# Three banks of one PSUM tile against three tiles of one bank each

## The chip, the cores and the metric

The kernel runs on one core of one Trainium2 chip. The metric is the device time in microseconds (us) of one execution; lower is better. The engines are TensorE (PE in the profile, with its weight loads apart as PEld), VectorE (DVE), ScalarE (ACT), GpSimd (POOL) and SyncE (SP, which issues the DMAs).

## What is computed

A chunked linear scan over 4 batches, 8 heads and 768 positions gives a matrix x of 3072 rows and 256 columns. Behind it stands a gated feed-forward block:

```python
y[:, :, sl] = y_intra + y_inter                   # scan, chunk by chunk
state = decay_full * state + np.sum(Bx, axis=2)
...
x = attn_out.transpose(0, 2, 1, 3).reshape(B * S, H * D)     # 3072 x 256
gate = 1.0 / (1.0 + np.exp(-(x @ w_gate)))        # w_gate, w_val: 256 x 1536
val = x @ w_val
return gate * val @ w_out                         # w_out: 1536 x 256
```

## The kernel before

Positions are taken in six chunks of 128 per batch. The scan of a chunk makes the chunk's columns of x, and the feed-forward block of an earlier chunk runs on TensorE meanwhile. Every fp32 product is made of three matmuls on operands that are split into a high and a low part (high by high, high by low, low by high).

The last two chunks are joined and are taken last. Their two feed-forward inputs are one block matrix of 2 x 2 blocks, and each product with a weight tile is made by a scheme of seven products instead of eight, on sums and differences of blocks (`joined_tasks`, L1456). There are twelve groups, `group(i)`, i from 0 to 11: the even ones multiply by w_gate, the odd ones by w_val. A group has seven products n of three matmuls of 128 x 512 each, all on L1362, in the order 1, 7, 2, 6, 4, 5, 3 (the last group: 1, 7, 6, 2, 5, 3, 4). Their moving operand tells them apart in the trace: products 1 and 2 are `gv<-x,w`, product 4 is `gv<-xt,w`, products 5, 6 and 7 are `gv<-xt,s`, product 3 is `gv<-xb,s`.

The products of a group go to three banks of PSUM, a, d and b. Products 1, 6, 5 and 3 are accumulated in a, products 7 and 4 in d, product 2 goes to b. Odd groups have a and b exchanged (`bank_of`, L1340), so that product 1 of a group goes to the bank that the group before leaves free. A group's results are read out by `corner(i, n)`:

- L1395, ACT: a copy out of the bank into a tile c, behind product 1 (corner 11), product 7 (corner 22) and product 6 (corner 21). The bank goes on being accumulated behind it.
- L1397, DVE: another bank is added to that copy, behind product 2 (b, corner 11), product 4 (d, corner 21) and product 5 (a, corner 22).
- L1400, ACT: the sigmoid of an even group's corner, in place. L1384, ACT: that of corner 12, straight out of the bank, behind product 3. L1388, DVE: corner 12 of an odd group, out of the bank times the sigmoid.
- L1404, DVE: an odd group's corner times the sigmoid.

`h_parts` splits each product of gate and value into two parts for the second matrix product (L1414, a cast on ACT or DVE; L1416, a subtraction on POOL or DVE), and `out_of` multiplies them by w_out (L1438, `acc<-w,h`, six matmuls of 256 columns a step, eight steps per two groups). `s_block(i)` makes the sums of weight blocks for group i: L1319 (`ww`, on POOL or DVE), L1326 (four of `sw`, DVE), L1329 (ACT), L1331 (POOL or DVE).

The order of the instructions on every engine is written out by hand in a list, `ORDER`, of entries such as `pe.group7` or `act.corner7_11`. Between engines, semaphores are placed by the framework, from the tiles that the instructions read and write: an instruction waits for those ahead of it in the program's order that touch the same tile. The three banks are slices of one tile of four banks, `gv`, which the pool `ps_cb` gives (L1358); that pool held the scan's tile of four banks before. So accesses to different banks of `gv` by different engines are kept in the program's order as well.

Of the kernel before, what the change touches and what calls it, by code (L numbers as in the profile page):

```python
# [8 lines left out]
F32 = mybir.dt.float32  # L9
# [5 lines left out]
PSUM = bass.MemoryType.PSUM  # L15
# [183 lines left out]
def tile_ssd_then_gated_ffn(  # L199
# [16 lines left out]
    P = 128  # L216
# [22 lines left out]
    dr = ctx.enter_context(tc.tile_pool(name="dr", bufs=1, space=DRAM))  # L239
    ps_mm = ctx.enter_context(tc.tile_pool(name="ps_mm", bufs=3, space=PSUM))  # L240
    ps_y = ctx.enter_context(tc.tile_pool(name="ps_y", bufs=1, space=PSUM))
    ps_cb = ctx.enter_context(tc.tile_pool(name="ps_cb", bufs=1, space=PSUM))


    ctx.enter_context(tc.manual_schedule(engines=None))
# [10 lines left out]
    for i in range(WARM):  # L256
        n = 4 if i < WARM - 1 else 3
# [59 lines left out]
    def step(eng, cost, needs=(), makes=(), port=False, **buffers):  # L317

        return eng, cost, needs, makes, port, buffers
# [928 lines left out]
    x7, s7, hj, bank, temps = {}, {}, {}, {}, {}  # L1248

    def x_part(name, part):  # L1250

        if name in ("b11", "b21"):
            if ("x5", part) not in x7:
                x7["x5", part] = wk.tile([P, NK, 512], F32R, tag=("xh", "xl")[part], name=f"x5{part}")
            return x7["x5", part][:, int(name == "b21")]
        if name not in x7:
            pool, tag = {"b22": (hp, "r0"), "t1": (wk, "xh"), "t2": (wk, "xl"), "t3": (wk, "bct"), "t4": (wk, "bct")}[name]
            x7[name] = pool.tile([P, 2, 512], F32R, tag=tag, name=f"x{name}")
        return x7[name][:, part]
# [73 lines left out]
    def standing(i, n):  # L1333

        if n in (1, 2, 4):
            k, f = {1: (0, 0), 2: (1, 0), 4: (1, 1)}[n]
            return [wgv[i][:, part, k, f * P : (f + 1) * P] for part in range(2)]
        return [s_part(i, part)[:, {5: 0, 6: 1, 7: 2, 3: 3}[n]] for part in range(2)]

    def bank_of(i, n):  # L1340

        return bank["gv"][:, "adb".index(n) if i % 2 == 0 or n == "d" else "bda".index(n)]

    def group(i):

        last = i - 1
        free = lambda k: [(k, last)] if i else []
        for n in (1, 7, 6, 2, 5, 3, 4) if i == NF - 1 else (1, 7, 2, 6, 4, 5, 3):
            needs = [("x7", MOVING[n], late) for late in range(2)] + ([("s7", i)] if n in (3, 5, 6, 7) else [])
            needs += {  # L1350
                1: free("b"), 7: free("d"), 2: free("a"), 6: [("s1", i)], 4: [("p7", i)], 5: [("u2", i)], 3: [("u4", i)]
            }[n]
            if i == 0:
                needs += [("sum", 2 * T1 + 1), ("pfirst", 2 * T1 + 1)]
            made = [("p", n, i)] + ([("done", i // 2)] if n == (4 if i == NF - 1 else 3) and i % 2 else [])
            yield step("pe", 3 * 0.227, needs, made, port=12)
            if "gv" not in bank:
                bank["gv"] = ps_cb.tile([P, 4, 512], F32, tag="pcb", name="gv")  # L1358
            out = bank_of(i, {1: "a", 6: "a", 5: "a", 3: "a", 7: "d", 4: "d", 2: "b"}[n])
            (wh, wl), (xh, xl) = standing(i, n), [x_part(MOVING[n], part) for part in range(2)]  # L1360
            for m, (one, two) in enumerate(((wh, xh), (wh, xl), (wl, xh))):
                nc.tensor.matmul(out, one, two, start=m == 0 and n in (1, 7, 2), stop=m == 2, skip_group_check=True)  # L1362
# [12 lines left out]
    def corner(i, n):  # L1375

        gate = i % 2 == 0
        free = [("free", nth(i, n) - 8)] if nth(i, n) > 7 else [("h", T2 - 1, f) for f in range(NF - 3, NF)]
        if (i, n) in ((0, "12"), (1, "11")):
            free += [("x7", k, late) for k in ("b22", "t1", "t2", "t3") for late in range(2)]  # L1380
        if n == "12":
            if gate:
                yield step("act", ACT_MM, [("p", 3, i)] + free, [("a", i), ("sig", i, n)])
                nc.scalar.activation(temp(i, n), bank_of(i, "a"), AF.Sigmoid)  # L1384
                return
            yield step("dve", DVE_MM, [("p", 3, i), ("sig", i - 1, n)], [("a", i), ("hf", i // 2, n)])
            g = temps[i - 1, n]
            nc.vector.tensor_tensor(out=g, in0=bank_of(i, "a"), in1=g, op=ALU.mult)  # L1388
            return
        product, of, copied, last, also, freed = {  # L1390
            "11": (1, "a", "s1", 2, "b", "b"), "22": (7, "d", "p7", 5, "a", "u4"), "21": (6, "a", "u2", 4, "d", "d"),
        }[n]
        yield step("act", ACT_MM, [("p", product, i)] + free, [(copied, i)])
        t = temp(i, n)
        nc.scalar.copy(t, bank_of(i, of))  # L1395
        yield step("dve", DVE_MM, [("p", last, i)], [(freed, i)])
        nc.vector.tensor_tensor(out=t, in0=bank_of(i, also), in1=t, op=ALU.add)  # L1397
        if gate:
            yield step("act", ACT_SB, [], [("sig", i, n)])
            nc.scalar.activation(t, t, AF.Sigmoid)  # L1400
            return
        eng = yield step(("dve", "pool"), (DVE_MM, 1.29), [("sig", i - 1, n)], [("hf", i // 2, n), ("free", nth(i, n))], port=True)
        g = temps[i - 1, n]
        engines[eng].tensor_tensor(out=g, in0=t, in1=g, op=ALU.mult)  # L1404
# [51 lines left out]
    def joined_tasks(t):  # L1456

        for late in range(2):
            for n in MOVING.values():
                task(t - 20.0 + 3 * late, f"x{n}_{late}", x_block(n, late))  # L1460
        for i in range(NF):
            at = t + 7.5 * i
            task(at - 12.0, f"s{i}", s_block(i))
            task(at, f"group{i}", group(i))
            for n, d in (("11", 0.9), ("22", 1.7), ("21", 3.0), ("12", 7.5)):
                task(at + d, f"corner{i}_{n}", corner(i, n))
        for j in range(NF // 2):
            for m, n in enumerate(PLACES):
                task(t + 15.0 * j + (11.0, 14.0, 16.0, 17.0)[m], f"part{j}_{n}", h_parts(j, n))
                task(t + 15.0 * j + (15.0, 18.0, 21.0, 24.0)[m], f"out{j}_{n}", out_of(j, n))  # L1470
        for k in (T2, T1):
            for at in range(2):
                task(t + 110.0 + (k == T1), f"rows{k}_{at}", stored_rows(k, at))
# [371 lines left out]
```

## Time and profile before

| | us |
|---|---|
| median of 3 runs (lowest to highest) | 407.23 (403.02 to 408.65) |
| the profiled execution, its own time | 404.01 |
| span of the profiled execution | 402.2 |
| TensorE busy | 361.2 (90%) |
| VectorE busy | 242.4 (60%) |
| ScalarE busy | 167.0 (42%) |
| GpSimd busy | 174.9 (43%) |

The span is the time from the first to the last instruction. Busy shares are means over stages of different kinds. Matmuls are pipelined, and the ends of a matmul are modelled: in rows of several, the distance of the starts tells the pace. The last stage runs from the first `gv` matmul at 251.87 us to the end of TensorE's work at 396.64 us.

### The profile page before, as it was taken

How to read it: one execution, taken by the hardware profiler on the slowest of the kernel's cores; microseconds unless marked ns; L12 is line 12 of the kernel's file. 1: busy time of each engine (PE TensorE's matmuls, PEld its weight loads, DVE VectorE, ACT ScalarE, POOL GpSimd, SP SyncE). 2: the span in 40 equal slices, each digit the busy share in tenths (PEclk: the TensorE clock that was granted, in tenths of full speed). 3: DMA queues.
4: the chain of work that ended last, by engine and by line, in shares of the span. 5: the costliest groups of instructions: out<-in, count | busy, mean ns of one | idle time of the engine just before them, and what ended most of it. 6: DMA issues, size and time to landing. Idle time of an engine off the chain costs nothing.

```text
span 402.2 us, 8260 instructions
## 1 busy us (share of the span) xinstructions
PE 361.2 (90%) x3328; PEld 279.9 (70%) x3328; DVE 242.4 (60%) x425; ACT 167.0 (42%) x315; POOL 174.9 (43%) x174
## 2 busy tenths in 40 slices
PE   8999999999999999999999997877778777787884
PEld 4676677878888888888888876546566655565674
DVE  7786878774467566552224589837495483818264
ACT  2577754368743135541044432432523333232321
POOL 5364776468975415662055464131362250302011
PEclk9999999999999999999999998999996999999999
DMA  8989844364624434420011000002000000000003
GB/s 169 266 201 256 292 137 117 76 100 117 132 75 95 93 73 80 113 55 13 18 38 29 15 2 2 0 1 45 9 0 0 0 2 0 0 2 0 0 2 104
DMA packets 87467, 27.43 MB, mean 68 GB/s; under 512 B 75718, under 2 KB 80262, under 8 KB 87430
## 3 DMA queue, kind: packets, MB, share of 16 engines
q1 hardware_dynamic: 82982, 26.26, 27.2%
q10 hardware_dynamic: 4448, 0.66, 1.0%
q8 instruction: 26, 0.43, 0.4%
q14 instruction: 11, 0.09, 0.1%
HBM read 23.46 MB, written 3.44 MB: 67 GB/s over the span
## 4 chain that ended last, share of the span: by engine, by line
PE 72%; DVE 14%; ACT 5%; issue 2%; POOL 1%; DMA 0%; DVEq 0%; ACTq 0%; POOLq 0%
PE gv L1362 15%; PE pg L1243 14%; PE pv L1243 14%; PE po L1497 9%; PE po L1535 6%; PE acc L1438 5%; ACT c L1395 4%; DVE c L1397 3%; DVE c L1404 2%; PE pv L1139 1%; PE banks L783 1%; PE banks L767 1%; PE pg L1139 1%; DVE h L1414 1%; DVE xt L1291 1%
## 5 line engine op out<-in xcount | busy, mean ns | idle before, releaser
L1210 POOL TENSOR_TENSOR h<-g,h 128x512 fp32r<-128x512 f32 x36 | 50.0, 1390 | 56.4 <-ACT h L1208 54.4
L1243 PE MATMUL pg<-xh,w 128*128 128x512 f32 x168 | 59.6, 395 | 0.0
L1243 PE MATMUL pv<-xh,w 128*128 128x512 f32 x168 | 58.9, 391 | 0.1
L1397 DVE TENSOR_TENSOR c<-gv,c 128x512 f32<-128x512 f32 x36 | 24.3, 688 | 55.7 <-PE gv L1362 42.6
L1497 PE MATMUL po<-h,w 128*128 128x512 f32 x216 | 52.1, 398 | 0.0
L1204 DVE TENSOR_TENSOR g<-pv,g 128x512 f32<-128x512 f32 x36 | 24.9, 691 | 41.9 <-PE pv L1243 40.9
L1497 PEld LDWEIGHTS po<-h,w 128*128 128x128 f32 x216 | 41.2, 192 | 9.0
L1416 POOL TENSOR_TENSOR h<-c,h 128x512 fp32r<-128x512 f32 x11 | 16.4, 1489 | 71.0 <-ACT h L1414 52.8
L1438 PEld LDWEIGHTS acc<-w,h 128*128 128x128 f32 x288 | 40.1, 195 | 3.6 <-DVE h L1416 0.4
L1362 PE MATMUL gv<-xt,s 128*128 128x512 f32 x108 | 33.7, 421 | 8.9 <-ACT c L1384 4.2
L1395 ACT COPY c<-gv 128x512 f32<-128x512 f32 x36 | 20.4, 587 | 51.0 <-PE gv L1362 46.3
L1438 PE MATMUL acc<-w,h 128*128 128x256 f32 x288 | 40.9, 287 | 0.2 <-DVE h L1416 0.2
L1183 ACT ACTIVATE g<-pg 128x512 f32<-128x512 f32 x44 | 26.3, 598 | 29.7 <-PE pg L1243 29.3
L1208 ACT CAST h<-g 128x512 fp32r<-128x512 f32 x35 | 21.7, 620 | 38.4 <-DVE g L1204 38.4
L1243 PEld LDWEIGHTS pg<-xh,w 128*128 128x128 f32 x168 | 31.5, 188 | 7.9 <-DVE h L1200 0.7
L1243 PEld LDWEIGHTS pv<-xh,w 128*128 128x128 f32 x168 | 31.5, 188 | 7.2 <-POOL w L495 0.5
L1243 PE MATMUL pg<-xl,w 128*128 128x512 f32 x84 | 32.7, 390 | 0.0
L1243 PE MATMUL pv<-xl,w 128*128 128x512 f32 x84 | 32.7, 389 | 0.0
L1362 PE MATMUL gv<-x,w 128*128 128x512 f32 x72 | 21.7, 410 | 11.2 <-ACT c L1395 10.1
L1362 PEld LDWEIGHTS gv<-xt,s 128*128 128x128 f32 x108 | 19.1, 192 | 17.8 <-ACT c L1384 6.8
L495 POOL TENSOR_TENSOR w<-wr,w 128x512 fp32r<-128x512 f32 x18 | 26.4, 1466 | 7.7 <-ACT w L493 4.9
L573 DVE TENSOR_TENSOR_SCAN ab<-ab,delta 128x512 f32<-128x512 f32 x20 | 27.1, 1359 | 3.9 <-DMA ab<-a_z 3.9
(182 smaller groups left out, 634.7 us busy)
## 6 DMA issues: line engine op xcount, KB each, us to landing
ab<-a_z SPq DMA_DIRECT2D x40, 128.0 KB
wr<-in_moe_w_gate_dram SPq DMA_DIRECT2D x6, 512.0 KB
wr<-in_moe_w_val_dram SPq DMA_DIRECT2D x6, 512.0 KB
wr<-in_moe_w_out_dram SPq DMA_DIRECT2D x6, 512.0 KB
xn<-in_x_dram SPq DMA_DIRECT2D x10, 256.0 KB
out_dram<-o SPq DMA_DIRECT2D x48, 32.0 KB
bn<-in_B_dram SPq DMA_DIRECT2D x10, 128.0 KB
out_dram<-o SPq DMA_DIRECT2D x10, 128.0 KB
```

Source lines behind the costliest of these rows:

```text
L495: engines[eng].tensor_tensor(out=lo, in0=lw, in1=hi.bitcast(F32), op=ALU.subtract)
L573: nc.vector.tensor_tensor_scan(out=t.rearrange("p h l -> p (h l)"), data0=t.rearrange("p h l -> p (h l)"), data1=delta.rearrange("p h l -> ...
L1183: nc.scalar.activation(gs[k, f], pm, AF.Sigmoid)
L1204: nc.vector.tensor_tensor(out=g, in0=pm, in1=g, op=ALU.mult)
L1210: engines[eng].tensor_tensor(out=hl, in0=g, in1=hh.bitcast(F32), op=ALU.subtract)
L1243: nc.tensor.matmul(pm, w[:, part, kt, fs], xx[:, kt], start=(i == 0), stop=(i == 3 * NK - 1))
L1362: nc.tensor.matmul(out, one, two, start=m == 0 and n in (1, 7, 2), stop=m == 2, skip_group_check=True)
L1395: nc.scalar.copy(t, bank_of(i, of))
L1397: nc.vector.tensor_tensor(out=t, in0=bank_of(i, also), in1=t, op=ALU.add)
L1438: nc.tensor.matmul(acc[:, k * DM : (k + 1) * DM], one(js), w[:, two, :], start=first and m == k == 0, stop=final and m == 2, skip_group_ch ...
L1497: nc.tensor.matmul(acc, w[:, part], hs[k, f][:, of_h], start=(f == 0 and i == 0), stop=(f == NF - 1 and i == 2))
L1535: nc.tensor.matmul(acc[:, :DM], hs[k, f][:, js], whole[NF + f // 2][:, f % 2], start=start, stop=stop, skip_group_check=True,)
```

## The change

The pool `ps_cb` gets an exit stack of its own, which is closed when the first group starts, and a new pool `ps_gv` gives three tiles of one bank, `gva`, `gvd` and `gvb`, in place of the three slices of `gv`. `bank_of` picks a tile from a list instead of a slice.

```diff
-    ps_cb = ctx.enter_context(tc.tile_pool(name="ps_cb", bufs=1, space=PSUM))
+    scan_banks = ctx.enter_context(ExitStack())
+    ps_cb = scan_banks.enter_context(tc.tile_pool(name="ps_cb", bufs=1, space=PSUM))
...
-        return bank["gv"][:, "adb".index(n) if i % 2 == 0 or n == "d" else "bda".index(n)]
+        return bank["gv"]["adb".index(n) if i % 2 == 0 or n == "d" else "bda".index(n)]
...
             if "gv" not in bank:
-                bank["gv"] = ps_cb.tile([P, 4, 512], F32, tag="pcb", name="gv")
+                scan_banks.close()
+                ps_gv = ctx.enter_context(tc.tile_pool(name="ps_gv", bufs=1, space=PSUM))
+                bank["gv"] = [ps_gv.tile([P, 512], F32, tag=n, name=f"gv{n}") for n in "adb"]
```

The instructions of each engine stand in the same order in both programs, with the line numbers three higher; what differs is what they wait for. TensorE, from product 7 to product 5 of group 7, before (`w7` are the weights of group 7, `s7` their sums, `x5` and `xt` parts of x):

```order
L1362 MATMUL gv_3230<-xt3_3031,s7_3596 128x512 [waits Activation_49]
L1362 MATMUL gv_3230<-xt3_3031,s7_3596 128x512 x2
L1438 MATMUL acc4_0_3436<-w14_1358,h2_12_3723 128x256 x6
L1362 MATMUL gv_3230<-x50_3111,w7_616 128x512 [waits Activation_49]
L1362 MATMUL gv_3230<-x51_3112,w7_616 128x512
L1362 MATMUL gv_3230<-x50_3111,w7_616 128x512
L1362 MATMUL gv_3230<-xt2_3136,s7_3596 128x512 x3
L1362 MATMUL gv_3230<-xt4_3142,w7_616 128x512 [waits DVE_49]
L1362 MATMUL gv_3230<-xt4_3142,w7_616 128x512 x2
L1438 MATMUL acc4_1_3446<-w14_1358,h2_12_3723 128x256 x6
L1362 MATMUL gv_3230<-xt1_3126,s7_3596 128x512 [waits DVE_49]
```

The same place in the changed program:

```order
L1365 MATMUL gvd_3235<-xt3_3031,s7_3602 128x512 [waits DVE_49]
L1365 MATMUL gvd_3235<-xt3_3031,s7_3602 128x512 x2
L1441 MATMUL acc4_0_3442<-w14_1358,h2_12_3729 128x256 x6
L1365 MATMUL gva_3234<-x50_3111,w7_616 128x512 [waits Activation_49]
L1365 MATMUL gva_3234<-x51_3112,w7_616 128x512
L1365 MATMUL gva_3234<-x50_3111,w7_616 128x512
L1365 MATMUL gvb_3236<-xt2_3136,s7_3602 128x512 [waits Activation_49]
L1365 MATMUL gvb_3236<-xt2_3136,s7_3602 128x512 x2
L1365 MATMUL gvd_3235<-xt4_3142,w7_616 128x512 [waits Activation_49]
L1365 MATMUL gvd_3235<-xt4_3142,w7_616 128x512 x2
L1441 MATMUL acc4_1_3452<-w14_1358,h2_12_3729 128x256 x6
L1365 MATMUL gvb_3236<-xt1_3126,s7_3602 128x512 [waits Activation_49]
```

Nothing moved; product 7 (`xt3`) now waits for DVE instead of ACT, product 4 (`xt4`) and product 5 (`xt1`) for ACT instead of DVE, and product 6 (`xt2`) has a wait of its own. ACT at the same place, before:

```order
L1384 ACTIVATE c6_12_3788<-gv_3230 128x512 [waits PE_49]
L1395 COPY c7_11_3793<-gv_3230 128x512 [waits PE_49,Pool_49]
L1395 COPY c7_22_3801<-gv_3230 128x512
L1395 COPY c7_21_3813<-gv_3230 128x512 [waits DVE_49,PE_49]
L1414 CAST h3_11_3823<-c6_11_3712 128x512 [waits DVE_49]
```

And in the changed program:

```order
L1387 ACTIVATE c6_12_3794<-gva_3234 128x512 [waits PE_49]
L1398 COPY c7_11_3799<-gvb_3236 128x512 [waits PE_49,Pool_49]
L1398 COPY c7_22_3807<-gvd_3235 128x512 [waits PE_49]
L1398 COPY c7_21_3819<-gvb_3236 128x512 [waits PE_49]
L1417 CAST h3_11_3829<-c6_11_3718 128x512 [waits DVE_49]
```

Here too nothing moved: each copy waits for TensorE alone or with POOL, and the copy of corner 21 no longer for DVE.

## Rows read from the trace of the kernel before

**Rows 1.** The chain that ended last, from 240 us on, by line.

```profile
by line: PE gv L1362 37.2%; PE acc L1438 12.6%; ACT c L1395 9.1%; DVE c L1397 8.4%; DVE c L1404 3.9%; DVE h L1414 2.9%; issue 2.8%; DVE xt L1291 2.6%; PE po L1497 2.5%; DVE h L1416 2.5%; DVE sw L1326 2.3%; ACT c L1384 2.2%; DVE c L1388 2.0%
```

**Rows 2.** TensorE's waits, 251 to 397 us: total us, times, longest us.

```profile
PE gv L1362 <- ACT c L1395: 12.3, 13, 2.1
PE gv L1362 <- DVE c L1397: 12.2, 15, 1.1
PE gv L1362 <- ACT c L1384: 4.2, 6, 0.7
```

**Rows 3.** Stretches of two groups: us; busy PE, PEld, DVE, ACT, POOL; clock; DMA.

```profile
251.80:273.40 21.60, 16.79 (x65) 11.16 (x64) 12.28 (x26) 7.98 (x14) 5.02 (x4) 1.00 0.00 0
273.40:296.00 22.60, 17.53 (x91) 13.61 (x89) 14.94 (x28) 9.44 (x17) 6.38 (x5) 1.00 0.12 24
296.00:321.40 25.40, 19.81 (x92) 15.63 (x90) 15.40 (x27) 8.53 (x16) 9.95 (x7) 0.87 0.00 0
321.40:344.80 23.40, 17.76 (x92) 13.73 (x91) 14.58 (x25) 8.13 (x15) 7.44 (x5) 1.00 0.00 1
344.80:367.50 22.70, 17.76 (x91) 13.72 (x90) 10.96 (x14) 6.95 (x12) 3.04 (x2) 1.00 0.00 1
```

**Rows 4.** Order of time on TensorE, 333 to 356: start, us, instruction, idle before.

```profile
333.11 0.96 PE L1362 MATMUL gv<-xb,s 128*128 128x512 f32 x3
...
335.45 0.96 PE L1362 MATMUL gv<-xt,s 128*128 128x512 f32 x3 [0.69 <-ACT c L1384]
...
337.63 0.96 PE L1362 MATMUL gv<-x,w 128*128 128x512 f32 x3 [0.51 <-ACT c L1395]
...
340.13 0.96 PE L1362 MATMUL gv<-xt,w 128*128 128x512 f32 x3 [0.85 <-DVE c L1397]
...
342.50 0.96 PE L1362 MATMUL gv<-xt,s 128*128 128x512 f32 x3 [0.69 <-DVE c L1397]
343.30 1.59 PE L1438 MATMUL acc<-w,h 128*128 128x256 f32 x12
344.80 0.96 PE L1362 MATMUL gv<-xb,s 128*128 128x512 f32 x3
345.60 0.86 PE L1362 MATMUL gv<-x,w 128*128 128x512 f32 x3
346.30 0.85 PE L1362 MATMUL gv<-xt,s 128*128 128x512 f32 x3
...
349.21 0.96 PE L1362 MATMUL gv<-x,w 128*128 128x512 f32 x3 [1.36 <-ACT c L1395]
...
351.72 0.96 PE L1362 MATMUL gv<-xt,w 128*128 128x512 f32 x3 [0.85 <-DVE c L1397]
...
355.82 0.98 PE L1362 MATMUL gv<-xb,s 128*128 128x512 f32 x3
```

**Rows 5.** Order of time on ACT and DVE in the same stretch: readers of gv.

```profile
334.80 0.60 ACT L1384 ACTIVATE c<-gv 128x512 f32<-128x512 f32 x1 [1.09 <-PE gv L1362]
...
336.50 1.07 ACT L1395 COPY c<-gv 128x512 f32<-128x512 f32 x2 [1.10 <-PE gv L1362]
...
339.39 0.69 DVE L1397 TENSOR_TENSOR c<-gv,c 128x512 f32<-128x512 f32 x1 [5.74 <-PE gv L1362]
...
347.18 0.58 ACT L1395 COPY c<-gv 128x512 f32<-128x512 f32 x1 [2.38 <-PE gv L1362]
```

**Rows 6.** The same stretch: DVE's operations on SBUF alone, and POOL's.

```profile
342.48 1.67 DVE L1404 TENSOR_TENSOR c<-c,c 128x512 f32<-128x512 f32 x1
...
344.88 1.75 POOL L1416 TENSOR_TENSOR h<-c,h 128x512 fp32r<-128x512 f32 x1 [1.28 <-ACT h L1414]
345.51 1.40 DVE L1414 CAST h<-c 128x512 fp32r<-128x512 f32 x1
...
348.52 0.43 DVE L1414 CAST h<-c 128x512 fp32r<-128x512 f32 x1
```

**Rows 7.** Order of time on TensorE: product 3 of group 10.

```profile
378.53 0.96 PE L1362 MATMUL gv<-xb,s 128*128 128x512 f32 x3
```

## The prediction

> **What bounds the kernel now.** I read the chain of waits first. Over the last 160 us its largest part, 37.2%, is TensorE's L1362 [rows 1], the seven products of the last stage; the same row holds L1395, L1397 and L1384, the instructions that read the three banks out. TensorE's own waits in that stage come next [rows 2]: it stood idle for 12.3 us behind L1395 (13 times), 12.2 behind L1397 (15) and 4.2 behind L1384 (6), 28.7 us in all. The table by stretches [rows 3] cuts the stage into pairs of groups: 21.6, 22.6, 25.4, 23.4 and 22.7 us. No other engine is full in any of them: DVE is busy for 10.96 to 15.40 us, ACT for at most 9.44, POOL for at most 9.95. So the pace is set by a hand-over between engines, not by an engine.
>
> The steady pair [rows 4] shows which hand-over. From product 3 of group 6 at 333.11 to product 3 of group 8 at 355.82 are 22.7 us. In flow, three matmuls of 512 columns take 0.70 (345.60 to 346.30), and twelve of 256 take 1.50 (343.30 to 344.80), so six take 0.75. A pair issues 42 and 48 of them: 14 x 0.70 + 8 x 0.75 = 15.8 us. The other 6.9 are six waits with the refill of the pipeline behind each.
>
> **What the change does to these six.** Group 6 has its banks in the order a, d, b; group 7 has a and b exchanged. The built program names the instruction whose signal each wait of rows 4 stands for.
> - 335.45, product 7 of group 7, writes d, and waits for L1384, which reads a.
> - 337.63, product 2, writes a, and waits for the copy out of d (the second of the two at 336.50, [rows 5]).
> - 340.13, product 4, writes d, and waits for the add at 339.39 [rows 5], which reads a.
> - 342.50, product 5, writes b, and waits for an add that reads d.
> - 349.21, product 2 of group 8, writes b, and waits for the copy out of d.
> - 351.72, product 4 of group 8, writes d, and waits for an add that reads b.
>
> All six are on another bank. The readers are held the same way: the copy of product 1 (b) at 336.50 starts 1.05 us behind the matmuls of product 7 (d). In the changed program each of these waits is for the last access of its own bank. No instruction is added, removed or moved on any engine, SP and POOL included; 24 more of TensorE's instructions and 6 more of ACT's raise a semaphore, and some matmuls wait on two. I take these at nothing: a wait already met leaves no gap in the flow of rows 4. The bound is 0.05 us on each of 84 products, 4 us.
>
> **The pair worked through with true waits alone.** Steps from rows 4 and 5: a reader starts 0.88 us behind the start of its three matmuls when they flow (346.30 to 347.18), a copy takes 0.58, an add 0.69, a sigmoid 0.60 (334.80), and a matmul follows a reader by 0.05 (copies end 337.57, product 2 at 337.63). Zero is the start of product 3 of group 6.
>
> Group 7 on TensorE in flow: product 1 at 0.70, 7 at 1.40, six acc, 2 at 2.85, 6 at 3.55, 4 at 4.25, six acc, 5 at 5.70, twelve acc, 3 at 7.90. ACT in its order: the sigmoid 0.88 to 1.48 (product 2 needs it: ready), the copy of product 1 until 2.16 (product 6 needs it), that of product 7 until 2.87 (product 4), that of product 6 until 5.02 (product 5). No wait so far. DVE: add 3.73 to 4.42, its product L1404 until 5.14, add 5.17 to 5.86, then a second L1404. That one takes 1.67 where POOL works beside it [rows 6], so until 7.56; the third add ends at 8.28, and product 3 starts at 8.33 instead of 7.90. Behind it DVE has L1404 until 9.0, the cast L1414 of 1.40 (0.43 without POOL, [rows 6]) until 10.43, a subtraction until 11.15 and L1388 until 11.87. Product 2 of group 8 needs L1388: it starts at 11.92, where flow would have it at 11.18. Product 5 of group 8 follows its copy, which stands behind a sigmoid on ACT, at 15.07 (flow: 14.77); twelve acc later product 3 of group 8 comes at 17.3. **The pair goes from 22.7 to 17.3**; of the 6.9 us, 5.4 go and 1.5 stay as true waits on DVE's late part.
>
> The other pairs by the same steps, with their own rows of DVE, ACT and POOL in program order:
> - groups 0 and 1 [rows 3]: DVE still makes s1 to s3 and delays product 3 of group 0 by 0.7; 21.6 to 15.9, gain 5.7.
> - groups 2 and 3: 22.6 to 16.6, gain 6.0; three waits of 0.2 to 0.3 stay.
> - groups 4 and 5: POOL's two ww at the head of group 4 stretch one more DVE operation by about 1 us, and product 2 waits 1.6. 18.4 against 25.4. The granted clock in this stretch is 0.87 [rows 3], and the pair is 2.0 to 2.8 us longer than its neighbours; with TensorE idle for less before it I let that dip go. Gain 7.0.
> - groups 6 and 7: the same head, 18.4 against 23.4, gain 5.0.
> - groups 8 and 9: 17.3 against 22.7, gain 5.4.
> - group 10: 9.0 against 11.0, gain 2.0.
> - the end, from product 3 of group 10 (378.53, [rows 7]): product 5 of group 11 comes 2.5 earlier, and DVE's chain behind it (add, L1404, cast, subtraction) then sets the start of the last acc; gain 2.7. What follows TensorE's end is the same.
>
> The sum is 33.8. Some 18 true waits stay, and three matmuls behind a wait take 0.1 longer than in flow (0.96 at 335.45 against 0.85 at 346.30, [rows 4]): minus 1.8. **Gain 32 us.** The profiled execution took 404.01, so 372. Its time stands 3.2 below the median of the runs, 407.23; I take 1 of this, for **373 us**.
>
> **How far this can be off.** Upper end of the gain: no wait at all would give 6.9 in each of 5.5 pairs and the 2.7 of the end, 41 us: 363. Lower end: DVE and POOL now work closer together, next paragraph.
>
> **Rivals.**
> - *DVE and POOL take the place of the false waits.* In a pair seven DVE operations have SBUF operands alone (three L1404, two casts, two subtractions). Those beside POOL take about 1 us more: 1.40 against 0.43 for the cast [rows 6]. My replay stretches two of seven in a light pair, four in a heavy one. If all seven stretch, 5 us more of DVE, of which some 3 lie in the chain from product 5 to product 2 of the next group: 20.3 per pair, gain 2.4 x 5.5 + 2.7 = 16, **388 us**. For it: POOL's subtraction took 1.75 in the same place [rows 6]. Against: POOL is busy 3.04 us in a light pair and at most 9.95 [rows 3]. The Trainium skill, page "SBUF — State Buffer", section "SBUF: two separate sides", says the same as a rule: VectorE with two SBUF inputs and GpSimd share a port pair that one of them locks for its whole instruction. By that rule a stretch can reach POOL's whole 1.28 to 1.75 us.
> - *The true chain on one bank holds the pace.* Product 1, copy, product 6, copy, product 5, add, product 3, sigmoid: 3 x 0.88 + 2 x 0.58 + 0.69 + 0.88 + 0.60 + 0.15 = 6.1 us per group, against 7.9 of issue. It would have to be 5 us longer for **404 to 408 us**, no change; nothing in rows 5 says so.
> - *Slower: the clock.* The dip to 0.87 lies in the stretch with the longest waits, up to 2.1 us [rows 2, 3]. If shorter bursts between short waits kept TensorE at the lower of its two levels (1.2 GHz) for half of the stage's 95 us of issue (12 x 7.9), this would cost 47 us against the 32: **419 us**. It decides from a third of the issue on. Against: all other stretches, with six waits a pair, show 1.00 [rows 3], and the change takes waits away. The Trainium skill, page "TensorE: Matmul & The Clock Gate", section "A second HAM failure mode: psum-queue depth-cycling", reports a kernel that cycled through banks and whose small idle times made the clock swing; by that rule this rival would be likelier than I make it, and rows 3 do not bear it out.
>
> **Chances.** The forecast, 364 to 383: 0.80. DVE and POOL, 383 to 396: 0.12. No change: 0.05. Slower: 0.03. The range that leaves two in ten out is **364 to 386**, lower end from no wait at all, upper end halfway into the first rival. Within 2% (about what a measurement of this kernel can tell from no change) means 399 to 415: faster 0.92, same 0.05, slower 0.03.
>
> **What the profile after would show.** TensorE's waits for L1395 and L1384 all but gone, those for L1397 and L1388 left at the heads of the even groups and before product 3, some 5 to 8 us in all instead of 28.7. Pairs of 16 to 18.5 us. DVE's busy share in them near 0.65 to 0.9, with more of its L1404, L1414 and L1416 stretched. Everything before 251.8 us unchanged. I am wrong if waits for ACT stay, if the pairs stay above 20 us, or if the granted clock falls in more than one stretch.

## The result and the profile after

The changed kernel takes 367.44 us (median of 6 runs, 365.88 to 368.73), the kernel before 404.18 us in the runs beside it (6 runs, 402.23 to 408.65). The ratio is 0.909, 95% interval 0.904 to 0.914: 36.7 us faster. The profiled execution took 366.27 us, its span is 364.5 us (before 402.2), so the two spans differ by 37.7 us. Lines of the changed kernel stand three further on: L1362 is now L1365, L1384 L1387, L1388 L1391, L1395 L1398, L1397 L1400, L1404 L1407, L1414 L1417, L1416 L1419 (in `e1` of the experiments one more, in `e2` and `e3` two more, so that L1400 is ScalarE's copy there).

Busy time and share of the span, and the chain that ended last by engine, from the page of after:

```profile
PE 346.8 (95%) x3328; PEld 277.5 (76%) x3328; DVE 241.2 (66%) x425; ACT 168.3 (46%) x315; POOL 178.0 (49%) x174
...
PE 63%; DVE 18%; DMA 5%; SPq 4%; issue 3%; ACT 1%; POOL 0%; DVEq 0%; POOLq 0%
```

The work is the same, and TensorE's share rose from 90% to 95%. In this chain, taken over the whole span, ScalarE is down to 1%; in the page of before it held 5%. TensorE's waits in the last stage of after (total us, times, longest us), to be held against [rows 2]:

```profile
PE gvb L1365 <- DVE c L1391: 4.1, 4, 1.8
PE gvd L1365 <- ACT c L1398: 1.4, 1, 1.4
PE gva L1365 <- ACT c L1398: 0.4, 2, 0.2
PE gva L1365 <- DVE c L1400: 0.3, 1, 0.3
PE acc L1441 <- DVE h L1419: 0.2, 1, 0.2
```

Before there were 36 waits of 30.1 us, 34 of them with 28.7 us for the three readers of [rows 2]. Nine waits of 6.4 us are left; 4.1 of these are for L1391 alone, at the heads of even groups. Stretches of two groups of after, cut from product 3 of an even group to the next (columns as in [rows 3], which are cut at the odd groups):

```profile
259.96:275.36 15.40, 15.40 (x78) 13.16 (x79) 12.05 (x21) 8.78 (x16) 6.55 (x5) 1.00 0.14 29
275.36:293.35 17.99, 15.98 (x93) 13.79 (x92) 16.12 (x31) 8.64 (x16) 11.35 (x9) 1.00 0.03 6
293.35:310.97 17.62, 15.92 (x92) 13.71 (x91) 15.47 (x28) 8.77 (x16) 10.03 (x7) 1.00 0.00 1
310.97:327.21 16.24, 15.81 (x93) 13.74 (x92) 10.94 (x16) 7.83 (x14) 3.50 (x2) 1.00 0.00 0
327.21:343.44 16.23, 15.80 (x92) 13.72 (x91) 10.21 (x14) 7.08 (x13) 3.44 (x2) 1.00 0.00 1
```

VectorE's busy share is now 0.63 to 0.90, and the granted clock is 1.00 in all of them. The steady pair that the prediction worked through [rows 4], on TensorE in after:

```profile
310.97 0.86 PE L1365 MATMUL gva<-xb,s 128*128 128x512 f32 x3
311.67 0.85 PE L1365 MATMUL gvb<-x,w 128*128 128x512 f32 x3
...
317.23 1.59 PE L1441 MATMUL acc<-w,h 128*128 128x256 f32 x12
318.66 0.86 PE L1365 MATMUL gvb<-xb,s 128*128 128x512 f32 x3
...
322.02 0.96 PE L1365 MATMUL gvb<-x,w 128*128 128x512 f32 x3 [0.43 <-DVE c L1391]
...
324.98 0.96 PE L1365 MATMUL gva<-xt,s 128*128 128x512 f32 x3
...
327.21 0.86 PE L1365 MATMUL gva<-xb,s 128*128 128x512 f32 x3
```

From product 3 of group 6 (310.97) to product 3 of group 7 (318.66) are 7.69 us with no wait at all; the second half loses 0.43 at product 2. Six waits were in this place before.

### The profile page after: what moved, and what is told of

It is laid out like the page before. It is cut to its first block, busy times and chain, and to the rows that moved or that the text cites. A ratio compares the mean times of both kernels' runs of the same rounds, so it can differ in the third digit from the quotient of the medians.

```text
span 364.5 us, 8267 instructions
## 1 busy us (share of the span) xinstructions
PE 346.8 (95%) x3328; PEld 277.5 (76%) x3328; DVE 241.2 (66%) x425; ACT 168.3 (46%) x315; POOL 178.0 (49%) x174
## 4 chain that ended last, share of the span: by engine, by line
PE 63%; DVE 18%; DMA 5%; SPq 4%; issue 3%; ACT 1%; POOL 0%; DVEq 0%; POOLq 0%
PE pg L1244 13%; PE pv L1244 13%; PE po L1500 10%; PE po L1538 6%; PE acc L1441 5%; PE gva L1365 4%; DVE c L1400 3%; DVE c L1407 3%; PE gvb L1365 3%; DVE h L1417 2%; PE gvd L1365 2%; DMA a_z<-a 2%; DMA wr<-in_moe_w_val_dram 2%; SPq L418 2%; PE banks L784 1%
## 5 line engine op out<-in xcount | busy, mean ns | idle before, releaser
L1211 POOL TENSOR_TENSOR h<-g,h 128x512 fp32r<-128x512 f32 x36 | 48.8, 1357 | 57.4 <-ACT h L1209 55.6
L1500 PE MATMUL po<-h,w 128*128 128x512 f32 x216 | 50.9, 391 | 0.0
L1500 PEld LDWEIGHTS po<-h,w 128*128 128x128 f32 x216 | 40.3, 188 | 8.6
L1441 PEld LDWEIGHTS acc<-w,h 128*128 128x128 f32 x288 | 38.7, 190 | 3.4 <-DVE h L1419 0.4
L1419 POOL TENSOR_TENSOR h<-c,h 128x512 fp32r<-128x512 f32 x11 | 19.0, 1741 | 43.2 <-ACT h L1417 29.7
L477 POOL TENSOR_TENSOR wr<-wr 128x512 int32<-128x512 int32 x18 | 20.4, 1138 | 12.6 <-ACT wr L475 7.7
L1538 PE MATMUL po<-wr,h 128*128 128x256 f32 x96 | 23.4, 394 | 0.1
L1332 POOL TENSOR_TENSOR s<-sw,s 128x512 fp32r<-128x512 f32 x8 | 10.8, 1362 | 22.8 <-ACT s L1330 22.8
L1538 PEld LDWEIGHTS po<-wr,h 128*128 128x128 f32 x96 | 17.6, 188 | 4.3 <-DVE h L1201 0.6
L1400 DVE TENSOR_TENSOR c<-gva,c 128x512 f32<-128x512 f32 x12 | 8.3, 690 | 18.8 <-PE gva L1365 18.7
```

What stands on the lines that cost most here:

```text
L477: nc.gpsimd.tensor_tensor(out=lw.bitcast(I32), in0=hw.bitcast(I32), in1=lw.bitcast(I32), op=ALU.add)
L1211: engines[eng].tensor_tensor(out=hl, in0=g, in1=hh.bitcast(F32), op=ALU.subtract)
L1441: nc.tensor.matmul(acc[:, k * DM : (k + 1) * DM], one(js), w[:, two, :], start=first and m == k == 0, stop=final and m == 2, skip_group_ch ...
L1500: nc.tensor.matmul(acc, w[:, part], hs[k, f][:, of_h], start=(f == 0 and i == 0), stop=(f == NF - 1 and i == 2))
L1538: nc.tensor.matmul(acc[:, :DM], hs[k, f][:, js], whole[NF + f // 2][:, f % 2], start=start, stop=stop, skip_group_check=True,)
```

## Experiments

**Theory A** is that of the prediction: the framework orders the accesses to a tile, so with one tile every product waits for the last access to any bank. **Theory C** is about the 6.4 us that are left: VectorE comes late to the heads of the even groups, and whatever is taken away there, the next hand-over behind VectorE holds TensorE instead. Ratios are to the kernel before on the same chip.

**1. One tile in the new pool** (`e1`). It tells the tile from the pool and its place in PSUM.

```diff
-                bank["gv"] = [ps_gv.tile([P, 512], F32, tag=n, name=f"gv{n}") for n in "adb"]
+                gv = ps_gv.tile([P, 4, 512], F32, tag="gv", name="gv")
+                bank["gv"] = [gv[:, n] for n in range(3)]
```

> The changed kernel, but the new pool gives one tile of four banks and the three banks are slices of it again. Theory A (the gain comes from the waits between different banks alone): all 47 waits of TensorE in the last stage return, 28 to 30 us of them, and the time is that of the kernel before, 402 to 406 us. Rival B (a good part comes from the new pool, its place in PSUM or its opening at the first group): the time stays below 395 us.

405.4 us, ratio 1.001 (0.998 to 1.005). TensorE's waits of this kernel:

```profile
PE gv L1366 <- ACT c L1399: 12.4, 13, 2.1
PE gv L1366 <- DVE c L1401: 12.2, 15, 1.1
PE gv L1366 <- ACT c L1388: 4.2, 6, 0.7
```

These are [rows 2] again, to 0.1 us and with the same counts: 34, where the 47 of the expectation counted waits of the readers for TensorE. The new pool, its place and the early end of the old one are worth nothing that these runs can tell (at most 0.5%); the gain is in the tiles.

**2 and 3. Two banks in one tile, the third apart** (`e2`: a and b share, `e3`: a and d share). The edit of `e2`; in `e3` `two` holds a and d, and `one` holds b:

```diff
-                bank["gv"] = [ps_gv.tile([P, 512], F32, tag=n, name=f"gv{n}") for n in "adb"]
+                two = ps_gv.tile([P, 2, 512], F32, tag="two", name="gvab")
+                one = ps_gv.tile([P, 512], F32, tag="one", name="gvd")
+                bank["gv"] = [two[:, 0], one, two[:, 1]]
```

> The changed kernel with banks a and b as slices of one tile of two banks and d as a tile of its own. The built program then holds the add of corner 11 of an even group until product 6 is done, so the sigmoid, the copy of corner 21 and product 5 behind it come about 0.7 to 1 us later in each even group; in odd groups the added waits are for work that is long done. Theory A: 5 to 6 even groups x 0.7 to 1 us, 371 to 374 us. Rival (each pair of banks that shares a tile costs a third of the gain, 12 us): about 380 us.

> The changed kernel with banks a and d as slices of one tile of two banks and b as a tile of its own. The built program brings back, in every pair of groups, the wait of product 7 for the sigmoid L1387 (0.7 plus 0.3 of refill), of product 2 for the copy out of d (0.4), of product 4 for the add out of a (0.3), and of product 5 of the even group for a copy that waits for product 4 (0.2). Theory A: about 2 us in each of 5.5 pairs, 376 to 381 us, and TensorE waits for ACT's sigmoid again, 3 to 4 us in all. Rival (a third of the gain for each sharing pair): about 380 us too, but then the run with a and b together reads the same.

Measured: 374.08 us, ratio 0.922 (0.917 to 0.927), a hair above the 371 to 374 forecast, and 376.46 us, ratio 0.928 (0.923 to 0.934), inside 376 to 381. Most of the gain comes with the first separation, either way, so it doesn't come in equal parts from the banks. The waits of `e2`, then of `e3`:

```profile
PE gvab L1367 <- DVE c L1393: 4.9, 4, 1.7
PE gvab L1367 <- ACT c L1400: 2.6, 5, 0.5
PE gvab L1367 <- DVE c L1402: 1.6, 3, 0.7
PE gvd L1367 <- ACT c L1400: 1.2, 1, 1.2
```

```profile
PE gvb L1367 <- DVE c L1393: 3.7, 4, 1.4
PE gvad L1367 <- ACT c L1400: 1.6, 3, 1.2
PE gvad L1367 <- DVE c L1402: 1.3, 5, 0.7
PE gvb L1367 <- DVE c L1402: 0.5, 1, 0.5
```

In `e2` the false wait between a and b is VectorE's, as forecast: in group 8 the add of corner 11 starts 0.89 us behind product 6 (329.44 and 328.55), in after 0.27 (323.09 and 322.82), and TensorE waits at product 5 for the copy behind it (four of the five waits for L1400). The odd groups, which I had at nothing, lose too: groups 5, 7 and 9 take 8.07 to 8.08 us instead of 7.68 to 7.69. `e3` is 9 us slower than the changed kernel, yet its list holds only 7.1 us of waits against 6.4, and the wait for the sigmoid that I expected isn't in it. The time is in the order of starts on TensorE; the same half pair that took 7.69 us above takes 9.02 in `e3` (the sigmoid on ScalarE first):

```profile
317.94 0.60 ACT L1389 ACTIVATE c<-gvad 128x512 f32<-128x512 f32 x1 [0.39 <-PE gvad L1367]
...
316.93 0.97 PE L1367 MATMUL gvad<-xb,s 128*128 128x512 f32 x3
317.74 0.86 PE L1367 MATMUL gvb<-x,w 128*128 128x512 f32 x3
318.59 0.96 PE L1367 MATMUL gvad<-xt,s 128*128 128x512 f32 x3
319.39 0.88 PE L1443 MATMUL acc<-w,h 128*128 128x256 f32 x6
320.23 0.97 PE L1367 MATMUL gvad<-x,w 128*128 128x512 f32 x3
321.03 0.86 PE L1367 MATMUL gvb<-xt,s 128*128 128x512 f32 x3
322.05 0.96 PE L1367 MATMUL gvad<-xt,w 128*128 128x512 f32 x3 [0.16 <-DVE c L1402]
...
325.95 0.96 PE L1367 MATMUL gvb<-xb,s 128*128 128x512 f32 x3
```

Four starts come late against the flow of after: 318.59 by 0.16 (0.85 behind the start ahead of it, where flow has 0.69), 320.23 by 0.13, 322.05 by 0.33 and 325.95 by 0.27. Behind each late start the next comes another 0.1 us later, as behind 316.93 here (0.81 instead of 0.70). That is 0.89 + 4 x 0.11 = 1.33, the whole difference, and only one of the four is listed as idle time, with 0.16. The first of them is the wait for the sigmoid: 318.59 is 0.05 behind its end (317.94 + 0.60), so it came back, for 0.16 us and not for the 0.7 of the expectation. A list of waits leaves out short ones, which the modelled ends cover; the distance of the starts doesn't.

**4. Corner 12 ahead on VectorE** (`e4`). In groups 3, 5, 7 and 9 L1391 stands ahead of the cast and subtraction of part 22, so that product 2 of the next group no longer waits behind them. For each of the four, in `ORDER`:

```diff
-dve.part1_22 ... dve.part1_22 ... dve.corner3_12 ... dve.part1_12
+dve.corner3_12 dve.part1_22 ... dve.part1_22 ... dve.part1_12
```

> The changed kernel, order of DVE alone changed: in groups 3, 5, 7 and 9 corner 12 (L1391) stands ahead of the cast and the subtraction of part 22 instead of behind them. TensorE's largest remaining wait is for L1391, 4.1 us in 4 times (longest 1.8). Theory C (what is left is DVE's chain in order: cast, subtraction, corner 12, cast, subtraction, then the add of corner 11 of the even group, on which ACT's sigmoid, the copy behind it and product 5 hang): the wait for L1391 goes, product 5 waits for ACT's copy instead, and the time stays within 1 us of 367. Rival D (the wait for L1391 is the price itself): 4 to 4.5 us faster, 363 us.

365.38 us, ratio 0.902 (0.896 to 0.908), between the two forecasts. The waits for L1391 are gone, and these came:

```profile
PE gva L1365 <- ACT c L1398: 4.3, 2, 2.3
```

Groups 4 and 6 gained nothing: product 5 waits 2.33 and 2.01 us for a copy that ScalarE makes behind the sigmoid of corner 11, which waits for VectorE's add. Groups 8 and 10 gained 0.7 us each, which I hadn't expected. VectorE and GpSimd in after, and behind that in `e4`, show why:

```profile
316.82 0.69 DVE L1407 TENSOR_TENSOR c<-c,c 128x512 f32<-128x512 f32 x1
316.87 3.50 POOL L1419 TENSOR_TENSOR h<-c,h 128x512 fp32r<-128x512 f32 x2 [6.29 <-ACT h L1417]
...
318.15 1.06 DVE L1407 TENSOR_TENSOR c<-c,c 128x512 f32<-128x512 f32 x1
319.25 1.40 DVE L1417 CAST h<-c 128x512 fp32r<-128x512 f32 x1
```

```profile
317.11 3.50 POOL L1419 TENSOR_TENSOR h<-c,h 128x512 fp32r<-128x512 f32 x2 [6.28 <-ACT h L1417]
...
320.41 0.49 DVE L1417 CAST h<-c 128x512 fp32r<-128x512 f32 x1
```

In after the cast begins at 319.25, inside GpSimd's second subtraction, which ends at 320.37; it ends at 320.65. In `e4` it begins at 320.41, 0.2 us before GpSimd's end (317.11 + 3.50 = 320.61), and takes 0.49. So the same cast costs 1.40 or 0.49 by when it begins.

**5. A fourth bank** (`e5`). The other way to free product 2: it writes into a fourth tile in the even groups, with no instruction moved. This and the next two ran beside the changed kernel itself (`c0`).

```diff
-                bank["gv"] = [ps_gv.tile([P, 512], F32, tag=n, name=f"gv{n}") for n in "adb"]
+                bank["gv"] = [ps_gv.tile([P, 512], F32, tag=n, name=f"gv{n}") for n in "adbe"]
...
-        return bank["gv"]["adb".index(n) if i % 2 == 0 or n == "d" else "bda".index(n)]
+        return bank["gv"][{"a": 0, "d": 1, "b": 3}[n] if i % 2 == 0 else {"a": 2, "d": 1, "b": 0}[n]]
```

> The changed kernel itself, beside the other three on one chip, so that differences of 1 us between them can be read. Every theory: 366 to 368 us, product 2 of groups 4 and 6 waits 1.8 and 1.5 us for the add of L1391.

> The changed kernel with a fourth tile in the pool, and product 2 of the even groups writing into it, so that it no longer waits until the add of L1391 has read bank b; no instruction is moved. If the wait for the bank is itself what 3.7 us of waits cost (theory D): 363 to 364 us. If it only shows that VectorE is late (theory C): product 2 is on time, and product 5 of groups 4 and 6 waits instead, since its bank is copied by ScalarE behind a sigmoid that waits for VectorE's add of the corner 11; the wait is 1.8 to 2.3 us in groups 4 and 6 and goes in groups 8 and 10 only by 0.4 each: 366 to 368 us.

The changed kernel: 367.26 us, ratio 0.906 (0.901 to 0.912). The fourth bank: 368.09 us, ratio 0.908 (0.902 to 0.915), no gain. In this execution group 4 ran in part at a lower clock (last section); groups 6, 8 and 10, without that, take 9.95, 8.52 and 8.54 us (to their product 3 from that of the group before), in the changed kernel beside it 9.93, 8.56 and 8.54. Product 2 is on time, and product 5 waits 5.5 us in four groups:

```profile
PE gva L1365 <- ACT c L1398: 5.5, 4, 2.3
```

The bank was never what was short (theory D falls): VectorE is late, as theory C has it.

**6 and 7. The next hand-overs in turn** (`e7`, `e8`). `e7` is `e4`, and on ScalarE the copy of product 6 stands ahead of that sigmoid in groups 4, 6, 8 and 10; in `e8` also the eight small additions of L1327 stand behind VectorE's add of corner 22 in groups 4 and 6.

```diff
-act.corner4_11 dve.s7 ... act.corner4_21 dve.s8 ... dve.corner4_22
+act.corner4_21 act.corner4_11 ... dve.corner4_22 dve.s7 dve.s8
```

> The kernel of the experiment before that put the corner 12 ahead on VectorE (365.4 us), and on ScalarE, in groups 4, 6, 8 and 10, the copy of product 6 ahead of the sigmoid of the corner 11 that waits for VectorE. Theory C: product 5 of groups 4 and 6 no longer waits (2.33 and 2.01 us there); the next limit is product 3 of these groups, which waits for the add of the corner 22, on VectorE behind the eight small additions of L1327, and loses 1.0 to 1.4 us of it again: 362.5 to 364 us. If the sigmoid was not what held the copy (ScalarE late in itself): 365 to 366 us as before. If nothing else is late: 361 us.

> The same, and in groups 4 and 6 the eight small additions of L1327 stand behind the add of the corner 22 on VectorE. Theory C: product 3 of groups 4 and 6 is then on time too, 1 to 1.4 us less for each: 361 to 362 us. Rival: VectorE's add now waits for product 5 with the additions behind it, and ScalarE's casts and GpSimd's subtractions of these weights come late for a later group: 363 to 365 us, with a wait of a product for the weights.

`e7` takes 363.94 us, ratio 0.898 (0.892 to 0.903), `e8` 363.03 us, ratio 0.896 (0.889 to 0.903), a little over the 361 to 362 forecast and at the lower edge of its rival's range, though no product waits for weights. In `e7` product 5 is on time and product 3 waits for the add, as forecast; its TensorE:

```profile
292.29 0.96 PE L1365 MATMUL gva<-xb,s 128*128 128x512 f32 x3 [1.52 <-DVE c L1400]
...
309.65 0.96 PE L1365 MATMUL gva<-xb,s 128*128 128x512 f32 x3 [1.50 <-DVE c L1400]
```

In `e8` that is gone too: groups 4 and 6 are 1.70 and 1.66 us shorter than in `e7`. But groups 5 and 7 are 1.28 and 1.07 longer, as product 7 waits for corner 21's add, which now stands behind the additions, and VectorE stays late behind it:

```profile
PE gvd L1365 <- DVE c L1400: 1.4, 2, 0.7
```

Against the changed kernel beside it `e8` is 4.2 us (1.2%) faster, with no overlap of their runs. It has the lowest median of all the kernels; its runs overlap with those of `e7`.

**8. A cast on ScalarE** (`e9`). From the changed kernel: in pairs 1 to 4 the cast of part 22 moves from VectorE to ScalarE.

```diff
-dve.part1_22 ... dve.part1_22
+act.part1_22 ... dve.part1_22
```

> The changed kernel with one kind of instruction moved: the cast of part 22 in pairs 1 to 4 (L1417, ahead of the add of L1391 for which product 2 of the next group waits) runs on ScalarE instead of VectorE. Naive theory: VectorE has 0.4 to 1.4 us less ahead of the add, so product 2 waits 0.4 to 0.5 us less in each pair: 365 to 366 us. Theory C (a VectorE instruction between SBUF tiles that begins while GpSimd works on SBUF is stretched, 0.43 to 1.40 and 0.69 to 1.67): the subtraction behind the cast now begins about where the cast stood, while GpSimd still works, and takes 1.67 us, in groups 8 and 10 too, where it took 0.69: product 2 of groups 4 and 6 gains about 0.6 us each, that of 8 and 10 loses about 0.4 each: 366.5 to 368 us.

365.15 us, ratio 0.903 (0.900 to 0.906): the naive forecast was right in the total, as groups 4, 6, 8 and 10 are each 0.42 to 0.47 us shorter than in after. Mine of 1.67 for the subtraction behind the cast was not right. In group 8 it took 1.01, as it began only 0.47 us before GpSimd's end (317.31 + 3.49 = 320.80); the row at 288.53 is of group 4:

```profile
288.53 1.67 DVE L1419 TENSOR_TENSOR h<-c,h 128x512 fp32r<-128x512 f32 x1
...
317.31 3.49 POOL L1419 TENSOR_TENSOR h<-c,h 128x512 fp32r<-128x512 f32 x2 [6.30 <-ACT h L1417]
...
320.33 1.01 DVE L1419 TENSOR_TENSOR h<-c,h 128x512 fp32r<-128x512 f32 x1 [0.69 <-ACT h L1417]
```

In groups 4 and 6 the wait of product 2 fell by 1.4 us each, three times the naive forecast, and product 5 took most of it back: its wait grew from 0.23 and 0.22 to 1.20 and 1.21 us. There the stretch of 1.67 came one subtraction later (288.53; 0.69 in after), ahead of the add that product 5 hangs on. So the hand-over behind VectorE took over again, as theory C has it.

**9. Two more hand-overs** (`e10`). `e8`, with ScalarE's copy of product 7 in group 0 ahead of its cast of weights, and the add of corner 21 in groups 4 and 6 ahead of the additions.

```diff
-act.s1 ... act.corner0_22 ... dve.corner4_22 dve.s7 dve.s8 act.s7 act.s8 ... dve.corner4_21
+act.corner0_22 act.s1 ... dve.corner4_22 dve.corner4_21 dve.s7 dve.s8 act.s7 act.s8
```

> The last of the kernels in better order (363.0 us), and in group 0 ScalarE's copy of product 7 ahead of its cast of the weights, in groups 4 and 6 VectorE's add of the corner 21 ahead of the eight small additions of L1327. Theory C: the wait of product 4 in group 0 (1.5 us) and of product 7 in groups 5 and 7 (0.7 us each) go: 360 to 361 us. Rival: the additions come late now, and a product of group 7 or 5 waits for its weights, or group 0 waits for the weights whose cast stands behind: 362.5 to 364 us.

364.96 us, ratio 0.903 (0.899 to 0.907). That is in the rival's range and 2 us above the median of `e8`, which ran on another chip; the two intervals overlap. The rival's mechanism isn't there: no product waits for weights. The waits aimed at are gone, and others stand one hand-over further on:

```profile
PE gva L1365 <- ACT c L1387: 3.0, 2, 1.5
PE gva L1365 <- DVE c L1400: 2.1, 1, 2.1
```

Product 2 of groups 5 and 7 waits 1.5 us for the sigmoid of L1387, which ScalarE reaches behind its casts of the late weights, and the two groups take 0.59 and 0.57 us more than in `e8`. Product 3 of group 0 now waits 2.09 us for VectorE, where it waited 0.33 in `e8`. It starts at 259.98, in after at 259.96: VectorE sets this start, and the wait of product 4 ahead of it had cost nothing. Group 1 behind it ran at a lower clock in this execution (last section), which added 1.6 us to it.

## Why the prediction was right, step by step

Forecast 373 us, measured 367.44; the gain came out at 36.7 us against 32.

- **Six false waits per pair.** Right. They are gone from the steady pair, and putting the banks back into one tile brings all of them back (`e1`).
- **The added signals at nothing.** Right as far as the flow shows it: products follow each other at 0.70 us in after (310.97 to 311.67), as in flow before.
- **The steady pair, 17.3.** Measured 16.24, 1.06 less. About 0.4 of that is the flow: half a pair without a wait takes 7.69 us, where I had 7.90. I had read twelve `acc` as 1.50 (343.30 to 344.80, [rows 4]), but product 3 came late there, as the next start 0.80 behind it shows (0.70 in flow); in after twelve take 1.43 (317.23 to 318.66). The other 0.6 is in the waits. The mis-sized term there is the second L1404 (now L1407), taken at 1.67 us as in [rows 6]. It took 0.69, as it begins at 316.82, 0.05 us before GpSimd's subtraction. So product 3 of group 7 isn't late (I had 0.43), product 2 of group 8 waits 0.43 (I had about 0.75), and product 5 starts only 0.06 late (I had 0.3). Two operations of the pair are stretched, as forecast, but they are the third L1407 (1.06) and the cast (1.40).
- **The other pairs.** Gains from the starts of product 3: groups 0 and 1 4.9 (forecast 5.7), 2 and 3 7.2 (6.0), 4 and 5 7.4 (7.0), 6 and 7 5.7 (5.0), 8 and 9 6.5 (5.4), group 10 2.4 (2.0), the end 2.7 (2.7): 36.8 in all against 33.8. The stage also begins 0.9 us earlier in this execution (first `gv` matmul at 250.95), which makes the 37.7 of the spans. I had everything ahead of the stage unchanged; its start is spread between executions: in `c0`, the same kernel, it begins at 253.19, behind a stretch at the lower clock (0.50 from 246 to 249, where after has 1.00), and product 3 of group 0 comes at 260.70 instead of 259.96.
- **The refill, minus 1.8 for some 18 waits.** Too much: nine waits are left, and the 36.8 holds their refill already. Of the 4.8 us by which the 32 was low, 3.0 are in the pairs, 1.8 in this term.
- **Group 0.** I had product 3 0.7 late; it is 0.31, but product 4 waits 1.44 us for ScalarE's copy, which stands behind a cast of weights that waits for VectorE. I had not followed that queue. It cost nothing: `c0` begins later, has no such wait (its list has 5.1 us), and `e10` shows that product 3 comes at the same time without it. So the 4.9 of groups 0 and 1 falls short of 5.7 by about the 0.9 of the earlier start, which was waited away here.
- **Heavy heads.** Right: I had a wait of 1.6 at product 2 of groups 4 and 6, and they are 1.78 and 1.49.
- **The clock's dip of 0.87 let go.** Right in this execution: 1.00 in all stretches of after. In before the dip cost 2.3 us: group 4 took 13.91 us (product 3 at 296.05 to product 3 at 309.96) and group 6, with the same two waits of 2.05 and 0.85 at full clock, 11.62.
- **The rivals.** VectorE and GpSimd don't hold a pair at 20.3; the pairs are 15.4 to 18.0, a little below the 16 to 18.5 forecast at their short end, and most of what VectorE still costs is in groups 4 and 6. A true chain on one bank holds nothing: half a pair runs through with no wait. The clock did not fall in the stage with the shorter waits in this execution; the mean clocks of the six runs are 0.983 to 0.998, so it falls somewhere in several of them, and no trace of those shows where.

The rule of the Trainium skill that stood behind the first rival (page "SBUF — State Buffer", section "SBUF: two separate sides": a VectorE instruction with two SBUF inputs, or in a two-port mode, and a GpSimd instruction take their shared port pair for a whole instruction, and the other waits) fits what these runs add. GpSimd's two subtractions in after, one by one, and its first one in before, where VectorE's L1404 began behind it (342.48, [rows 6]):

```profile
316.87 1.80 POOL L1419 TENSOR_TENSOR h<-c,h 128x512 fp32r<-128x512 f32 x1 [6.29 <-ACT h L1417]
318.63 1.73 POOL L1419 TENSOR_TENSOR h<-c,h 128x512 fp32r<-128x512 f32 x1
...
342.31 1.28 POOL L1416 TENSOR_TENSOR h<-c,h 128x512 fp32r<-128x512 f32 x1 [9.71 <-ACT h L1414]
```

The stretched cast of after ends 0.28 to 0.29 us behind the end of a GpSimd instruction; the stretched L1407 of after and the subtraction of `e9` both end 0.54 behind one. Each is a little less than the instruction's own time (0.43, 0.69, 0.69). The L1407 that began 0.05 us ahead of GpSimd's kept its 0.69, and there GpSimd's took 1.80 instead of 1.28. So the stretch is what is left of the other engine's instruction, not a fixed 1 us, and it goes both ways; the prediction should have placed both engines in time instead of carrying the 1.67 of one place over. The adds out of PSUM (L1400) kept 0.68 to 0.69 beside GpSimd. The cast has one SBUF input only; whether it ran in a two-port mode, no run shows.

Left open: VectorE's lateness was moved about by order alone, and GpSimd's work itself was never taken away, so the part that it has in VectorE's lateness is read from the traces and not shown by an experiment of its own.

## What to carry to other kernels

A dependence that is tracked by tile joins banks that have nothing to do with each other: give each bank that several engines hand over a tile of its own, and read in the built program which instruction a wait really stands for before you look for a late engine. Behind that, count the time between starts on the engine that sets the pace, as waits of 0.1 to 0.3 us mostly don't show as idle time. Once most waits are gone, moving one instruction ahead is worth only the distance to the next hand-over: the waits of 2.33 and 2.01 us that the sixth experiment took away shortened their groups by 0.9 and 0.5.

## What the runs showed of the hardware

The granted clock can fall to the lower level (0.50, 1.2 GHz) behind a wait of TensorE, and needn't. In `e5` product 5 of group 4 waited 2.33 us and behind it one stretch reads (columns as in [rows 3]):

```profile
292.00:293.00 1.00, 1.00 (x5) 0.89 (x4) 0.24 (x1) 0.59 (x1) 1.00 (x1) 0.50 0.00 0
```

The twelve `acc` matmuls there took 2.74 us instead of 1.60, and group 4 took 11.86 us. In `e4` the same product waited 2.33 us as well, the clock stayed at 1.00, and the group took 10.36. In `e10` it fell behind the wait of 2.09 in group 0, and group 1 took 9.21 us from product 3 to product 3 at a mean clock of 0.81, where after had 7.61. In before it fell behind the wait of 2.05 in group 4 and not behind that of 2.05 in group 6.

It doesn't take one long wait. In `e1` the clock also fell behind four waits of 0.69, 0.68, 0.68 and 0.85 us in group 1, which in before, at the same places and equal to 0.01, left it at 1.00:

```profile
271.00:273.00 2.00, 2.00 (x6) 1.52 (x6) 1.38 (x2) 1.04 (x2) 0.00 (x0) 0.50 0.00 0
```

So a fall cost 1.5 and 1.6 us more than the wait itself in `e5` and `e10`, and what decides whether it comes could not be told from these runs.
